# One of eight first-round passes computes its softmax on transposed scores

## The chip, the cores and the metric

The kernel runs on one core of one Trainium2 chip. The metric is the device time of one execution in microseconds; three runs of the kernel before gave 825.45, 827.18 and 828.26 us, so the median is 827.18 us. The engines are named as in the profile: PE (TensorE; PEld are its weight loads), DVE (VectorE), ACT (ScalarE), POOL (GpSimd), SP (SyncE, which issues the DMAs).

## The reference, cut to what matters

```python
# q, k, v: (4, 8, 1152, 64) float32; factor 2, scale 1/8
q_pool = q.reshape(B, H, 576, 2, 64).mean(axis=3)
scores = scale * np.matmul(q_pool, k.transpose(0, 1, 3, 2))      # 576 x 1152 for each head
scores = scores - np.max(scores, axis=-1, keepdims=True)
attn = np.exp(scores)
attn = attn / (np.sum(attn, axis=-1, keepdims=True) + 1e-09)
x = np.matmul(attn, v)                                           # heads side by side: (2304, 512)
out = ((x @ w_a) * (x @ w_b)) @ w_out                            # w_a, w_b: 512 x 1536; w_out: 1536 x 512
```

## The kernel before, in words

Attention is done in passes. A pass is one pair of heads of one batch, and the two heads lie in the two halves of the 128 partitions (64 dimensions each). Batch 0 is done in two rounds: four passes over the 256 "even" queries of each pair, then four over the other 320; the later batches take each pair in one pass. A block is 128 queries of one head: its scores are a row of 1152 numbers on each of 128 partitions, in the accumulator `sps`, which has room for the two heads' blocks and no more.

For a block, DVE scales the scores, takes the row maximum and copies them to a buffer `s` in one instruction (`sm_max`, L734); ACT writes exp(s - max) and the row sum (`sm_exp`, L741); DVE forms the reciprocal of the sum (L745, L751). What follows depends on the pass. In the first four passes (`N_PE = 4`, the first round of batch 0) the exponentials stay in float32: PE transposes them in 36 blocks of 128 x 128 a pass into the two accumulators `ab` (`tr_pe`, L776), ACT and DVE copy them out (`tr_out`, L787 and L789), PE multiplies them with v (`pv_f`, L820), and ACT and DVE divide by the sums with the help of a small diagonal matrix (`r_diag` L792, `r_wide` L796, `x_copy` L870, `r_mul` L800). In all later passes the probabilities are split into two float16 parts (L754, L758) and transposed by DMA.

Beside the first eight passes, all the weights are prepared. There are 36 tiles of 512 KB; each is loaded, two ACT instructions (`w_tail` L592, `w_abs` L573) and one on POOL (`w_sign` L596) take its bits apart, DVE joins them (`w_join` L603), its largest magnitude is found (`w_mag`, on ACT L582 or on DVE L585), PE adds the magnitudes over partitions into `xps` (`w_sum` L615), and ACT and DVE write a high and a low part (`w_hi` L639, `w_lo` L643 to L652). After the even round of batch 0 its 256 tokens go through the two expert products (`moe_mm` L944), which a last `w_sum` precedes on PE, and from then on attention of later batches alternates on PE with the expert tiles.

The order is not left to a scheduler: five lists of task numbers (`ORDERS`), one for each engine, give the sequence in which each engine executes its tasks, and each engine executes its queue strictly in order. `add` records what each task reads and writes, and a task waits until those before it on the same names are done.

Of the kernel before, what the change touches and what calls it, by code (L numbers as in the profile page):

```python
# [18 lines left out]
NP = H // 2  # L19
# [12 lines left out]
K_PART = 640  # L32
N_PE, EVICT = 4, "ADADA"
# [276 lines left out]
def kernel(  # L310
# [41 lines left out]
    osb = [T(f"o{u}", [128, DM]) for u in range(2)]  # L352
    z_t = osb + [T("z2", [128, 512])]
    one = T("one", [128, 1])
    vmx = T("vmx", [128, NPAIR])

    vsc = T("vsc", [128, NPAIR, 4])
    vb = T("vb", [128, B, 2])
# [847 lines left out]
```

## Time and profile before

| what | value |
|---|---|
| median of three runs | 827.18 us (825.45 to 828.26) |
| the profiled execution, whole | 824.38 us |
| its span, first to last instruction | 822.6 us |
| PE busy, mean granted clock | 782.5 us (95%), 0.979 |
| DVE busy | 615.3 us (75%) |
| ACT busy | 581.9 us (71%) |
| POOL busy | 246.6 us (30%) |

The shares are means over two very different stretches. The chain that ended last runs through PE for 74% of the span, but of the 40 slices of the profile (20.6 us each) PE is below 90% in the first six, and ACT and DVE are near full there. A granted clock of 1.00 is 2.4 GHz on TensorE and 0.50 is 1.2 GHz, so 0.75 over a stretch means half of it at the lower level.

### The profile page before, as it was taken

The numbers are of one execution on the slowest core, as the hardware profiler recorded it, in microseconds if no ns is written. First come the engines' busy times: TensorE is split into PE (matmuls) and PEld (weight loads), VectorE is DVE, ScalarE is ACT, GpSimd is POOL, SyncE is SP. The second block draws the span as 40 slices with busy tenths as digits, with TensorE's granted clock in tenths as the row PEclk, the third lists the DMA queues.
The fourth block names the chain that finished last, engine by engine and source line by source line (L and its number), as shares of the span: only waits on it lengthen the run. The fifth ranks groups of instructions, "written<-read, shape, count | busy, mean of one in ns | idle before, by whom it ended". The sixth has DMA issues, their size and how long they took to land.

```text
span 822.6 us, 21334 instructions
## 1 busy us (share of the span) xinstructions
PE 782.5 (95%) x8880; PEld 605.2 (74%) x8880; DVE 615.3 (75%) x1180; ACT 581.9 (71%) x986; POOL 246.6 (30%) x226
## 2 busy tenths in 40 slices
PE   8888569999999999999999999999999999999997
PEld 5665347776777767777777777887788888887886
DVE  5988999897799899999999999989977423022110
ACT  6999999887877788788887878778857452233212
POOL 5667876234201143111322023102300220402203
PEclk9988689999999999999999999999999999999999
DMA  8555688999999999999999999999958314000100
GB/s 306 205 199 182 194 212 254 185 209 222 202 200 221 214 201 190 199 201 217 202 209 195 174 159 190 193 186 186 182 103 141 76 43 100 2 27 1 27 2 26
DMA packets 316433, 132.32 MB, mean 161 GB/s; under 512 B 300848, under 2 KB 302896, under 8 KB 316336
## 3 DMA queue, kind: packets, MB, share of 16 engines
q1 hardware_dynamic: 316336, 130.96, 76.0%
q8 instruction: 69, 1.13, 0.6%
q14 instruction: 28, 0.23, 0.1%
HBM read 50.72 MB, written 4.72 MB: 67 GB/s over the span
## 4 chain that ended last, share of the span: by engine, by line
PE 74%; DVE 11%; ACT 8%; DMA 4%; issue 2%; SPq 1%; DVEq 0%; POOL 0%; ACTq 0%; POOLq 0%
PE ab L944 30%; PE ab L970 16%; PE xps L857 10%; PE sps L699 8%; PE sps L702 7%; DVE s L734 3%; DMA pt<-p 3%; DVE p L758 2%; ACT s L741 2%; PE xps L820 1%; ACT p L754 1%; DMA vraw<-in_v_dram 1%; DMA xt<-in_w_ab_dram 1%; ACT xt L592 1%; ACT pt L787 1%
## 5 line engine op out<-in xcount | busy, mean ns | idle before, releaser
L944 PEld LDWEIGHTS <-wab 128*128 128x128 f16 x2592 | 251.5, 98 | 32.7 <-issue 2.1
L944 PE MATMUL ab<-xt,wab 128*128 128x256 f16 x2304 | 260.7, 273 | 1.3 <-DVE o L976 0.8
L741 ACT ACTIVATE s<-s,st 128x1152 f32<-128x1152 f32 x144 | 180.0, 1250 | 28.9 <-DVE s L734 28.1
L758 DVE SCALAR_TENSOR_TENSOR p<-s,st,p 128x1152 f16<-128x1152 f32 x128 | 183.5, 1438 | 11.9 <-ACT p L754 11.5
L964 POOL TENSOR_TENSOR gl<-g,gh 128x256 fp32r<-128x256 f32 x108 | 90.1, 839 | 321.6 <-ACT gh L961 293.3
L754 ACT ACTIVATE p<-s,st 128x1152 f16<-128x1152 f32 x128 | 159.3, 1249 | 36.8 <-DMA pt<-p 11.4
L970 PE MATMUL ab<-wo,gh 128*128 128x512 f32 x432 | 139.5, 404 | 2.0 <-DVE g L956 1.7
L951 ACT ACTIVATE g<-ab,cc 128x256 f32<-128x256 f32 (+1 forms) x144 | 55.1, 415 | 83.7 <-PE ab L944 83.1
L734 DVE TENSOR_SCALAR_CACHE_REDUCE s<-sps,ksc 128x1152 f32<-128x1152 f32 x72 | 101.0, 1409 | 13.5 <-PE sps L702 13.1
L699 PE MATMUL sps<-k,q 64*128 64x512 f32 (+3 forms) x448 | 101.4, 546 | 9.6 <-DVE s L734 4.8
L956 DVE SCALAR_TENSOR_TENSOR g<-ab,cc,g 128x256 f32<-128x256 f32 (+1 forms) x144 | 55.2, 410 | 74.0 <-ACT g L951 73.8
L857 PEld LDWEIGHTS <-vs 128*64 128x64 f16 x3888 | 100.4, 110 | 13.0 <-issue 11.0
L857 PE MATMUL xps<-pt,vs 128*64 128x128 f16 (+1 forms) x3888 | 109.0, 215 | 0.7 <-DMA pt<-p 0.5
L734 DVE TENSOR_SCALAR_CACHE_REDUCE s<-sps 128x1152 f32<-128x1152 f32 x72 | 96.7, 1349 | 15.4 <-PE sps L699 14.5
L699 PEld LDWEIGHTS sps<-k,q 64*128 64x128 f32 (+1 forms) x448 | 47.6, 183 | 63.3 <-issue 53.2
L970 PEld LDWEIGHTS ab<-wo,gh 128*128 128x128 f32 x432 | 78.1, 188 | 20.5 <-issue 1.8
L970 PE MATMUL ab<-wo,gl 128*128 128x512 f32 x216 | 85.5, 396 | 1.0 <-POOL gl L964 1.0
L961 ACT ACTIVATE gh<-g 128x256 fp32r<-128x256 f32 x108 | 43.9, 411 | 55.3 <-PE ab L970 50.6
L702 PE MATMUL sps<-k,q 64*128 64x512 f16 (+3 forms) x624 | 65.5, 341 | 1.7 <-DVE s L734 1.6
L702 PEld LDWEIGHTS <-q 64*128 64x128 f16 (+1 forms) x720 | 36.7, 97 | 40.9 <-issue 8.3
L596 POOL TENSOR_SCALAR xt<-xt 128x512 f16<-128x512 f32 x22 | 51.9, 2360 | 27.1 <-ACT xt L592 20.8
L976 DVE COPY o<-ab 128x512 f32<-128x512 f32 x9 | 6.2, 687 | 64.0 <-PE ab L970 64.0
(124 smaller groups left out, 763.9 us busy)
## 6 DMA issues: line engine op xcount, KB each, us to landing
k<-in_k_dram SPq DMA_DIRECT2D x18, 576.0 KB, 4.6
vraw<-in_v_dram SPq DMA_DIRECT2D x17, 576.0 KB, 4.6
xt<-in_w_ab_dram SPq DMA_DIRECT2D x15, 512.0 KB, 3.8
qraw<-in_q_dram SPq DMA_DIRECT2D x12, 576.0 KB, 4.9
out_dram<-o SPq DMA_DIRECT2D x16, 256.0 KB, 2.9
xt<-in_w_out_dram SPq DMA_DIRECT2D x7, 512.0 KB, 3.7
g<-in_w_ab_dram SPq DMA_DIRECT2D x5, 512.0 KB, 3.3
wab<-in_w_ab_dram SPq DMA_DIRECT2D x4, 512.0 KB, 3.9
```

Of the source, the lines that this page charges most:

```text
L699: nc.tensor.matmul(out, q, k, start=True, stop=True)
L702: nc.tensor.matmul(out, q[:, hq], k[:, hk], start=(hq, hk) == (0, 0), stop=(hq, hk) == (1, 0))
L734: nc.vector.tensor_scalar(out=s_t[sbuf(i)], in0=sps[:, at:at + S], scalar1=-1.0 / 16.0 if u is None else ksc[:, u, 4:5], scalar2=None, op0 ...
L741: nc.scalar.activation(out=s, in_=s, func=AF.Exp, scale=-1.0, bias=t[:, 0:1], accum_out=t[:, 1:2])
L754: nc.scalar.activation(out=p_t[pbuf(i)][:, 0], in_=s_t[sbuf(i)], func=AF.Copy, scale=st_t[i % NST][:, 3:4])
L758: nc.vector.scalar_tensor_tensor(out=p[:, 1], in0=s, scalar=st_t[i % NST][:, 3:4], in1=p[:, 0], op0=ALU.mult, op1=ALU.subtract)
L857: nc.tensor.matmul(xps[half(e), at:at + w], vs[:, c, e, hv], pt[t][:, hp, c, c0:c0 + w], start=(c == 0 and n == 0), stop=(c == NCH - 1 and ...
L944: nc.tensor.matmul(dst if t < 8 else dst.rearrange("p (b n) -> p b n", b=B), wab[:, f, 1 - m, a, c], moe_x(t, b, c), start=(n == 0), stop= ...
L951: nc.scalar.activation(out=g_t[:, f, c], in_=ab[j][:, 1, c], func=AF.Copy, scale=cc[:, b, f, 0:1])
L956: nc.vector.scalar_tensor_tensor(out=g, in0=ab[j][:, 0, c], scalar=cc[:, b, f, 1:2], in1=g, op0=ALU.mult, op1=ALU.mult)
L964: nc.gpsimd.tensor_tensor(out=gl_t[j], in0=g_t[:, f], in1=gh_t[j].bitcast(F32), op=ALU.subtract)
L970: nc.tensor.matmul(acc[u], g[:, us], wo[:, f, a], start=(first and n == 0), stop=(last and n == 2))
```

## The change

The second pass of the first round (`T_PASSES = (1,)`, heads 2 and 3 of batch 0, even queries) gets a routine of its own, `t_pass`, in place of the four blocks. It still forms the four blocks of scores as before, but DVE only takes their maxima (`t_max`). Four small products with the identity lay the 4 x 128 maxima along the free dimension (`t_row`), and ACT keeps them in a row (`t_keep`). Then the scores are formed a second time, transposed, with keys on the partitions, in five groups (chunks of 128 keys: 2, 2, 2, 2, 1): for each chunk and head one product of k and q and one of a selecting matrix `sel` with the maxima, which subtracts the maximum in the accumulator (`t_s`). ACT writes the exponentials of a group out of both accumulators (`t_exp`), and these are the operands of p times v without any transpose; a product with ones forms the row sums in the other half of `xps` (`t_pv`, which begins with a product of zeros over all of `xps`). At the end ACT copies the sums, DVE takes reciprocals and multiplies (`t_sum`, `t_rec`, `t_out`). For this pass the 36 transposes and their copies, the exponentials by rows, the diagonals and `r_wide` are gone. The exponentials lie in the buffers `p` and in two of the six `pt` slots. POOL fills `sel` at the very start. All five order lists are new.

```diff
+T_PASSES, T_SLOTS = (1,), (4, 5)
...
+    def t_max(i):
+        at = S_AT[blocks[i].head]
+        nc.vector.tensor_reduce(out=st_t[i % NST][:, 0:1], in_=sps[:, at:at + S], axis=AX.X, op=ALU.max)
+
+    def t_row(i0):
+        for r in range(2):
+            for e in range(2):
+                m = st_t[(i0 + 2 * r + e) % NST][:, 0:1]
+                nc.tensor.matmul(
+                    xps[half(e), 128 * r:128 * r + 128], m.broadcast_to([128, 64]), ident, start=True, stop=True
+                )
+
+    def t_s(ps_, j, g):
+        for n, c in enumerate(GROUPS[g]):
+            for e in range(2):
+                nc.tensor.matmul(
+                    acc[e][:, TOK * n:TOK * n + TOK], kn[ps_.jk][half(e), 128 * c:128 * c + 128],
+                    qs[ps_.jq][half(e), 0:TOK], start=True, stop=False,
+                )
+            for e in range(2):
+                nc.tensor.matmul(acc[e][:, TOK * n:TOK * n + TOK], sel[half(e)], mrow[half(e)], start=False, stop=True)
+
+    def t_exp(j, g, e):
+        n = len(GROUPS[g])
+        nc.scalar.activation(
+            out=room(j, g, e)[0], in_=acc[e][:, 0:TOK * n], func=AF.Exp, scale=1.0 / 16.0
+        )
+
+    def t_pv(p, j, g):
...
+            for e in range(2):
+                nc.tensor.matmul(xps[half(e), 0:TOK], vf[p % 2][:, c, 64 * e:64 * e + 64], at[e][:, TOK * n:TOK * n + TOK], start=False, stop=False)
+            for e in range(2):
+                nc.tensor.matmul(xps[half(e), TOK:2 * TOK], one.broadcast_to([128, 64]), at[e][:, TOK * n:TOK * n + TOK], start=False, stop=stop)
...
+        add("PE", 0.5, i - 10, t_row, (ps_.base,), r=[f"st{k % NST}m" for k in range(ps_.base, i)] + ["g0"], w=["xps"], mode=2)
+        add("ACT", 0.27, i - 4, t_keep, (j,), r=["xps"], w=["g4"])
+        for g, of in enumerate(GROUPS):
...
+            add("PE", 0.04 + 0.88 * w, i - 7 + g / 5, t_s, (ps_, j, g), r=kq_names(ps_) + ["g3", "g4"], w=["acc0", "acc1"], mode=1)
...
+        if m in T_PASSES:
+            t_pass(ps_, m)
```

ACT's queue at the second pass, before. L787 are copies of transposes, L741 exponentials, L792 diagonals, L870 the copy of p times v, and the lines on `wab`, `z`, `g` and `xt_64` are weights:

```order
L787 ACTIVATE pt_71<-ab_105 128x512
L792 ACTIVATE g<-g,st 128x128
L741 ACTIVATE s_82,st<-s_82,st 128x1152
L592 ACTIVATE wab<-wab 128x512
L573 ACTIVATE z_96<-g 128x512
L592 ACTIVATE g<-g 128x512
L582 ACTIVATE wab,wmx<-wab 128x512
L787 ACTIVATE pt_72<-ab_105 128x512
L592 ACTIVATE xt_64<-xt_64 128x512
L741 ACTIVATE s_80,st<-s_80,st 128x1152
```

The same queue now, up to the first exponentials of the transposed pass (L855 is `t_keep`, L869 `t_exp`, L753 an exponential of the third pass, L651 `w_hi`, L603 `w_tail`, L988 the split of the first pass's result):

```order
L651 ACTIVATE wab<-o_95,wsc 128x512
L593 ACTIVATE wab,wmx<-wab 128x512
L651 ACTIVATE wab<-o_94,wsc 128x512
L584 ACTIVATE o_95<-wab 128x512
L651 ACTIVATE wab<-wab,wsc 128x512
L855 ACTIVATE g<-xps 128x256
L603 ACTIVATE xt_64<-xt_64 128x512
L988 ACTIVATE xt_63<-x_66 128x256
L753 ACTIVATE s_82,st<-s_82,st 128x1152
L869 ACTIVATE p_86<-ab_106 128x512
L869 ACTIVATE p_86<-ab_107 128x512
```

Weight conversions now stand where the second pass had its exponentials and copies, and `t_keep` follows them.

PE's queue at the second pass, before: the pass's last scores (`k_73,q_79`), transposes into `ab`, two `w_sum` (L615), and the third pass's scores (`k_74,q_78`) between them:

```order
L699 MATMUL sps<-k_73,q_79 128x128
L776 MATMUL ab_106<-g,s_80 128x128 x4
L615 MATMUL xps<-wmx,one 128x2
L776 MATMUL ab_105<-g,s_80 128x128 x4
L615 MATMUL xps<-wmx,one 128x2
L699 MATMUL sps<-k_74,q_78 128x512 x4
L699 MATMUL sps<-k_74,q_78 128x128
```

PE's queue now, from the same last scores to the first of the transposed ones (L627 is `w_sum`, L850 `t_row`, L860 and L865 `t_s`):

```order
L711 MATMUL sps<-k_73,q_79 128x128
L627 MATMUL xps<-wmx,one 128x2 x2
L711 MATMUL sps<-k_74,q_78 128x512 x4
L711 MATMUL sps<-k_74,q_78 128x128
L627 MATMUL xps<-wmx,one 128x2
L850 MATMUL xps<-g,st 64x128 x4
L860 MATMUL ab_106<-q_79,k_73 128x256
L860 MATMUL ab_107<-q_79,k_73 128x256
L865 MATMUL ab_106<-g 128x256
```

The small products with the maxima stand behind the third pass's first scores and behind a third `w_sum`.

## Rows read from the trace of the kernel before

**Rows 1.** Busy time by stretch: range, length, PE, PEld, DVE, ACT, POOL, clock, DMA.

```profile
8.27:38.00 29.73, 26.06 (x208) 18.42 (x207) 26.89 (x62) 29.41 (x62) 21.62 (x11) 1.00 0.77 283
38.00:61.70 23.70, 19.36 (x147) 14.52 (x146) 20.49 (x47) 21.75 (x46) 16.41 (x10) 0.86 0.53 184
61.70:95.00 33.30, 26.76 (x177) 16.32 (x176) 30.02 (x68) 32.32 (x64) 27.80 (x16) 0.81 0.57 195
95.00:121.40 26.40, 13.52 (x116) 8.75 (x114) 25.82 (x47) 24.60 (x46) 19.90 (x10) 0.72 0.82 204
121.40:200.00 78.60, 76.72 (x976) 57.75 (x974) 67.85 (x120) 67.51 (x108) 32.61 (x25) 1.00 1.03 215
200.00:700.00 500.00, 497.24 (x6404) 386.91 (x6405) 424.78 (x777) 371.60 (x563) 101.13 (x115) 1.00 0.93 175
```

**Rows 2.** Chain that ended last, before the expert products: start, us, engine, tile, line.

```profile
119.75 1.23 ACT wab L582 x4
121.03 0.38 PE xps L615 x2
```

**Rows 3.** Timeline of ACT: start, length, engine, line, operation, shapes.

```profile
30.94 1.25 ACT L741 ACTIVATE s<-s,st 128x1152 f32<-128x1152 f32 x1
...
32.18 0.36 ACT L870 ACTIVATE x<-xps,vsc 128x128 f32<-128x128 f32 x1
32.43 0.69 ACT L792 ACTIVATE g<-g,st 128x128 f32<-128x128 f32 x2
33.02 0.43 ACT L787 ACTIVATE pt<-ab 128x128 f32<-128x128 f32 x2
33.33 0.68 ACT L592 ACTIVATE xt<-xt 128x512 int32<-128x512 uint32 x1
33.90 0.42 ACT L894 ACTIVATE xt<-x 128x256 f16<-128x256 f32 x1
34.20 0.59 ACT L787 ACTIVATE pt<-ab 128x512 f32<-128x512 f32 x1
34.68 1.34 ACT L639 ACTIVATE wab<-o,wsc 128x512 f16<-128x512 f32 x2
```

**Rows 4.** Timeline of ACT, an exponential's high part and its successor.

```profile
98.55 1.29 ACT L754 ACTIVATE p<-s,st 128x1152 f16<-128x1152 f32 x1
99.69 0.69 ACT L573 ACTIVATE o<-xt 128x512 f32<-128x512 f32 x1
```

**Rows 5.** Timeline of DVE, end of the second pass's maxima.

```profile
28.59 1.36 DVE L734 TENSOR_SCALAR_CACHE_REDUCE s<-sps 128x1152 f32<-128x1152 f32 x1
...
30.60 0.68 DVE L789 COPY pt<-ab 128x512 f32<-128x512 f32 x1
31.19 0.67 DVE L585 TENSOR_REDUCE wmx<-o 128x1 f32<-128x512 f32 x1
...
31.86 0.69 DVE L603 SCALAR_TENSOR_TENSOR z<-z,g 128x512 int32<-128x512 int32 x1
32.57 0.29 DVE L800 SCALAR_TENSOR_TENSOR x<-x,xps 128x128 f32<-128x128 f32 x1
32.78 1.35 DVE L734 TENSOR_SCALAR_CACHE_REDUCE s<-sps 128x1152 f32<-128x1152 f32 x1
```

**Rows 6.** Timeline of PE at the full clock, second pass.

```profile
26.36 2.20 PE L699 MATMUL sps<-k,q 64*128 64x512 f32 x10 [0.40 <-DVE s L734]
...
28.49 1.09 PE L776 MATMUL ab<-g,s 128*128 128x128 f32 x8
...
29.51 2.19 PE L820 MATMUL xps<-pt,vs 128*64 128x128 f32 x36
...
31.52 0.39 PE L796 MATMUL xps<-g,one 128*64 128x128 f32 x4
```

**Rows 7.** Timeline of PE, the same two products later.

```profile
52.28 3.66 PE L820 MATMUL xps<-pt,vraw 128*64 128x128 f32 x36
...
65.03 4.15 PE L699 MATMUL sps<-k,q 64*128 64x512 f32 x10 [0.15 <-DVE s L734]
```

More of the change, by code (lines that the diff above doesn't have):

```diff
@@ L396, with room @@
     ptf = [x.rearrange("p a c n -> p (a c n)").bitcast(F32).rearrange("p (c n) -> p c n", c=NCH) for x in pt]
+    sel, mrow, rsum = g_t[:, 3, 0:128], g_t[:, 4], g_t[:, 5]
+    GROUPS = [range(c, min(c + 2, NCH)) for c in range(0, NCH, 2)]
+    spare = [(x.rearrange("p a n -> p (a n)").bitcast(F32), [f"p{j}h", f"p{j}l"]) for j, x in enumerate(p_t)]
+    spare += [(pt[j].rearrange("p a c n -> p (a c n)").bitcast(F32), [f"pt{j}"]) for j in T_SLOTS]
+    spare = [(x[:, 512 * n:512 * n + 512], names) for x, names in spare for n in range(2)]
+    def room(j, g, e):
+        x, names = spare[2 * g + e if g < 4 else 8]
+        return x[:, 256 * e:256 * e + 256] if g == 4 else x, names
     vf = [vs.rearrange("p c e h d -> p (c e h d)").bitcast(F32).rearrange("p (c n) -> p c n", c=NCH), vraw]
@@ new lines, in t_keep @@
+    def t_keep(j):
+        nc.scalar.activation(out=mrow, in_=xps[:, 0:TOK], func=AF.Copy)
+    def t_s(ps_, j, g):
[7 more added lines that the diff above has]
+                nc.tensor.matmul(acc[e][:, TOK * n:TOK * n + TOK], sel[half(e)], mrow[half(e)], start=False, stop=True)
@@ new lines, in t_exp @@
+    def t_exp(j, g, e):
[4 more added lines that the diff above has]
+    def t_pv(p, j, g):
+        at = [room(j, g, e)[0] for e in range(2)]
+        if g == 0:
+            for e in range(2):
+                nc.tensor.matmul(
+                    xps[half(e)], zero.broadcast_to([128, 64]), zero.broadcast_to([128, 2 * TOK]), start=True, stop=False
+                )
+        for n, c in enumerate(GROUPS[g]):
+            stop = c == NCH - 1
+            for e in range(2):
+                nc.tensor.matmul(xps[half(e), 0:TOK], vf[p % 2][:, c, 64 * e:64 * e + 64], at[e][:, TOK * n:TOK * n + TOK], start=False, stop=False)
+            for e in range(2):
+                nc.tensor.matmul(xps[half(e), TOK:2 * TOK], one.broadcast_to([128, 64]), at[e][:, TOK * n:TOK * n + TOK], start=False, stop=stop)
@@ new lines, in t_sum, with t_rec, t_out, t_pass @@
+    def t_sum():
+        nc.scalar.activation(out=rsum, in_=xps[:, TOK:2 * TOK], func=AF.Copy, bias=1e-9)
+    def t_rec():
+        nc.vector.reciprocal(out=rsum, in_=rsum)
+    def t_out(p, j, x0):
+        nc.vector.scalar_tensor_tensor(
+            out=x32[j][:, x0:x0 + TOK], in0=xps[:, 0:TOK], scalar=vb[:, p // NP, 1:2] if p % NP == NP - 1 else vsc[:, p, 0:1], in1=rsum, op0=ALU.mult, op1=ALU.mult
+        )
+    def t_pass(ps_, n):
+        j, i, p = 0, ps_.base, ps_.p
+        for rows, *_ in ps_.todo:
+            for e in range(2):
+                scores(ps_, i, rows, e)
+                ps_.last_max = add("DVE", 1.27, i - 4, t_max, (i,), r=[f"sps{e}"], w=[f"st{i % NST}m"])
+                i += 1
+        add("PE", 0.5, i - 10, t_row, (ps_.base,), r=[f"st{k % NST}m" for k in range(ps_.base, i)] + ["g0"], w=["xps"], mode=2)
+        add("ACT", 0.27, i - 4, t_keep, (j,), r=["xps"], w=["g4"])
+        for g, of in enumerate(GROUPS):
+            w = len(of)
+            add("PE", 0.04 + 0.88 * w, i - 7 + g / 5, t_s, (ps_, j, g), r=kq_names(ps_) + ["g3", "g4"], w=["acc0", "acc1"], mode=1)
+            for e in range(2):
+                add("ACT", 0.06 + 0.21 * w, i - 4 + g / 5, t_exp, (j, g, e), r=[f"acc{e}"], w=[f"room{j}{g}{e}"])
+            add("PE", 0.04 + 0.88 * w + 0.25 * (g == 0), i - 9 + g / 5, t_pv, (p, j, g), r=[f"room{j}{g}{e}" for e in range(2)] + [x for e in range(2) for x in room(j, g, e)[1]] + vbuf(p) + ["ones"],
+                w=["xps"], mode=2)
+        add("ACT", 0.27, i - 5, t_sum, (), r=["xps"], w=["g5"])
+        add("DVE", 0.33, i - 5, t_rec, (), w=["g5"])
+        add("DVE", 0.4, i - 5, t_out, (p, ps_.jx, XE), r=["xps", "g5", f"vb{p // NP}" if p % NP == NP - 1 else f"vsc{p}"], w=[f"x32{ps_.jx}{c}" for c in range(XE // 64, (XE + TOK) // 64)])
+        x_split(ps_, ("even",), i - 4)
@@ L1095 @@
     add("POOL", 0.8, -30, unity, (), w=["g0"], port=False)
+    add("POOL", 0.6, -25, select, (), w=["g3"], port=False)
     for n in range(IDLE):
@@ L1111, in attend @@
             prep_qk(nxt, nxt.base - 6)
+        if m in T_PASSES:
+            t_pass(ps_, m)
+            if nxt and not nxt.again:
+                prep_vmax(nxt.p, nxt.parts[0] == "even", ps_.end - 4)
         i = ps_.base
-        for r, (rows, (at, w), leaving, splits) in enumerate(ps_.todo):
+        for r, (rows, (at, w), leaving, splits) in enumerate(ps_.todo if m not in T_PASSES else ()):
             slots = []
```

5 lines of the change are left out of this document (added), and 287 rows, old and new, of the table ORDERS.

## The prediction, made before the changed kernel ran

> **What bounds the kernel now.** I read the busy times by stretch first. From 121.4 to 700 us PE is busy 574.0 of 578.6 us at a clock of 1.00, so whatever starts the expert products earlier or later moves the end by as much. Before 121.4 us PE is busy in parts only and the clock falls to 0.72. ACT is the fullest engine there: 29.41 of 29.73 us, then 21.75 of 23.70, 32.32 of 33.30 and 24.60 of 26.40; it waits 5.05 us of 113.1 from its first instruction at 8.27 us. DVE is near full too but waits 9.9 us in the same four rows [rows 1]. The chain of waits names the hand-over: ACT takes two weight magnitudes until 120.98, PE adds them up and starts the expert products at 121.4 [rows 2]. So the question is when ACT has worked off its queue up to that last magnitude. ACT executes in order; a wait early in the queue is not made good by work that stands behind it.
>
> **The change part by part.** I take the cost on ACT as the distance from one start to the next, since its instructions overlap at the ends: an exponential of 1152 is 1.24 us, a copy of p times v 0.25, a diagonal 0.295, a pair of small copies 0.31, a weight conversion 0.57, a 512-wide copy out of an accumulator 0.48, a high weight part 0.61 [rows 3], a high part of 1152 is 1.14 [rows 4].
>
> ACT loses 4 exponentials (4.96), 4 wide copies (1.92), 2 pairs of small ones (0.62), 4 diagonals (1.18) and 2 copies of p times v (0.50): 9.2 us. It gains 8 exponentials 512 wide, 2 of 256 and two copies of 256. No row shows an exponential out of an accumulator: the wide copy (0.48) bounds it from below, 512/1152 of 1.24 from above (0.55). I take 0.50, nearer to the copy, 0.30 for 256: 5.2 us, 5.0 to 5.6. Net **-4.0 us of ACT work** ahead of the expert products.
>
> DVE's four maxima stay at one pass over 1152 each (1.29 from 28.59 to the next) [rows 5]; what goes is 4 wide copies of 0.60, small sums and products, about 3.5, and a reciprocal and a product of 256 come in. No row shows a wide reciprocal. At DVE's rate of 1152 in 1.29 us the two take about 0.65; if a reciprocal is several times slower per element, 2.5. I take 0.7, since nothing but the pass's own result waits for it. Net -2.8.
>
> PE loses 36 transposes (0.13 each, from 28.49 to 29.51 for 8), two p times v (2.01) and two `r_wide` (0.3): 9.3 us [rows 6]. Five score products of 2176 columns in all take 2.13 us, 0.98 ns a column. The pass adds 36 products of 256 columns in `t_s` and as many in `t_pv`: 9.0 us each at that rate, 8.0 at that of p times v (18 x 128 columns in 2.01). With `t_row` and the zeros it is 17.5 to 18.7; if the two heads' products did not overlap in the new shapes it would be twice that. I take 18. Net **+8.7 us of PE**, in a stretch where PE is busy 45.4 of 53.4 us up to 61.7 [rows 1]. It costs nothing by itself: ACT is the limit and PE has room; the cover goes where ACT waits for a group. The POOL fills lie ahead of the first q sum, in the wait for its load; SP issues the same loads in a new order.
>
> If ACT waited as long as now, its 4.0 us less would be the gain. But the new routine adds a wait in front of everything it does: **no exponential can be formed before all four maxima are taken**, where the old pass started each block's exponential after its own maximum. I walk through the queues with the durations above.
>
> *First wait.* The scores of a pass come block after block, because `sps` holds two, and between the maxima DVE still has the first pass's copies and the joins. The third and fourth maximum start at 28.6 and 32.8 now [rows 5]. With the new order I get 29.5 and 32.8, so the fourth again ends at 34.1. DVE's 22.0 us of work up to there would allow 29, but PE and DVE wait for each other over `sps`. Behind the last maximum PE's queue has, ahead of `t_row`, the third pass's scores (2.1) and a `w_sum` that waits for two magnitudes on DVE (about 37.5, behind a join that needs ACT). So `t_row` ends at 38.4 and `t_keep` starts at 38.65. ACT's queue up to it holds 14 weight conversions, 4 exponentials, 6 magnitudes and high parts, 8 copies of transposes, 4 diagonals and 2 of p times v: 20.85 us. From 8.27 it could be through at 29.1. **It waits 9.5 us where it now waits 0.3** in that stretch [rows 1].
>
> *Second wait.* From `t_keep` to `t_sum` ACT has 19.8 us to do (11 conversions, 7 weight parts, 3 exponentials of the third pass, the 10 of this one, 2 copies, a split). Each group of `t_s` (1.8 us) writes both accumulators, so it waits for both exponentials of the group before, and these stand between weight work in ACT's queue. PE in the same time has 18 us of this pass, the third pass's scores (2.6) and transposes (1.8). Walking both queues I find 2.6 us in which ACT waits for a group. `t_sum` ends at 61.75.
>
> *What is left.* From there to the last magnitude before the expert products ACT's queue holds 33 conversions, 11 exponentials of 1152, 6 other passes over 1152, 23 weight parts and magnitudes, 8 diagonals, 4 copies of p times v, 3 splits and 14 copies of transposes: 61.6 us. Now ACT does 56.9 us from 61.7 to 121.4 and waits 2.8 [rows 1]. So it is **4.7 us behind**. I give back 1.8 of the 2.8 us of waits, since an engine that is behind finds what it needs ready more often, and DVE has some 3 us less to do; 1.0 stays. The last magnitude then ends at 124.4 against 120.9, and the expert products start 3.5 us later.
>
> From there both orders hold the same work on PE, which is full [rows 1], so the 3.5 us reach the end. The profiled execution took 824.38 us (span 822.6); it would be 827.9. It lies 2.8 us under the median of the three runs, and I carry that over: **830.7 us**. The waits give the forecast's own range: with none in the transposed stage the shift is 0.9, with all of 2.8 kept it is 5.3, and an error of 1.5 us in the walk comes on top, so 828.5 to 834.
>
> **The rivals.** *The gain is kept.* The order lists put the stage where ACT has other work at hand, ACT waits 5 us in all as now, and the 4.0 us come through: 823.2. For it: ACT was full and is the engine relieved. Against it: the order puts 20.85 us of ACT work in front of `t_keep`, and the fourth maximum cannot come much before 34.
>
> *A wash.* The first wait is as I say or a few us shorter, the stage runs without waits, and ACT later never waits: work left at the sums 2 us smaller than I count, shift about 0: 827. For it: the four rows sum to only 5.05 us of ACT waits now, so a well-packed queue is possible. Against it: DVE is at 95% or more over 95 to 121 and would have to be ahead.
>
> *The clock falls in the transposed stage* and the change costs much more. Now, whenever PE works in pieces with waits between, the same products take 3.66 us instead of 2.19 and 4.15 instead of 2.20 [rows 6, 7], and the clock of that stretch is 0.86. The new stage is such work: five groups of 1.8 us, each waiting for two exponentials. If half of its 18 us ran at 1.2 GHz, the groups on ACT's path would grow by about 4.5 us in all: 835. Against it: PE has more to do there than now, and where it is full the clock is 1.00. The Trainium skill, TensorE: Matmul & The Clock Gate, section "A second HAM failure mode: psum-queue depth-cycling", says that a PE that cycles through PSUM banks and idles shortly between groups oscillates between its two clocks; by that rule this rival would be the likely one, and the trace agrees so far as its pieces of work between 52 and 69 us ran at the low level.
>
> **How the numbers follow.** A measurement of this kernel tells a change of about 0.3% (2.5 us) from none. Forecast: 0.52, seven eighths of it over 829.7. Gain kept: 0.17. Wash: 0.25, all of it within 0.3%. Fallen clock: 0.06. So faster is 0.17, same 0.25 and an eighth of 0.52, 0.32, and slower the rest of 0.52 and 0.06, 0.51. The range runs from 824 to 834.5: it leaves out most of the gain and the upper half of the fallen clock, under 2 in 10.
>
> **What would show it.** In the changed kernel's profile: `t_keep` near 38.6 us with ACT idle 8 to 10 us before it, released by PE's products with the maxima; the sums' copy near 62; two waits or more of ACT for PE inside the stage; the expert products from 124 to 126; PE full and at 1.00 from there. I am wrong if ACT's idle time up to the start of the expert products stays under 8 us, or if that start comes at 121.4 or earlier. If the start is as I say and the end isn't, then PE was not what bound the rest.

## The result: 11.3 us slower, and the profile after

The changed kernel took 837.93 us in the median (837.01 to 840.40, four executions) against 826.62 us for the kernel before on the same chip (825.45 to 828.26, four). The recorded ratio is 1.0142, with a 95% interval of 1.0117 to 1.0167 (it is not the ratio of the two medians, which is 1.0137). I had forecast 3.5 us slower and a range that ended at 834.5. The direction was right; the size was not, and the time lies outside the range. The rivals that kept the gain or made it a wash are out. The profiled execution took 837.39 us, its span is 835.6 us (before 822.6): 13.0 us more.

Busy time by stretch of the changed kernel, columns as in [rows 1]; the last row is the stretch from the sums of the new pass to the first expert product.

```profile
8.27:38.00 29.73, 24.40 (x179) 16.32 (x178) 26.30 (x51) 21.25 (x43) 17.31 (x9) 0.94 0.59 217
38.00:61.70 23.70, 22.58 (x182) 15.20 (x181) 15.27 (x24) 20.13 (x40) 16.41 (x9) 1.00 0.54 187
61.70:95.00 33.30, 25.11 (x190) 16.83 (x188) 30.88 (x73) 30.66 (x64) 23.13 (x14) 0.95 0.48 168
95.00:121.40 26.40, 13.65 (x84) 9.29 (x80) 26.01 (x49) 25.39 (x46) 19.04 (x10) 0.61 0.84 244
...
200.00:700.00 500.00, 493.70 (x6324) 381.28 (x6323) 425.76 (x778) 373.63 (x567) 104.87 (x118) 1.00 0.93 176
61.70:128.60 66.90, 44.46 (x327) 29.88 (x324) 64.09 (x129) 63.00 (x123) 48.30 (x26) 0.82 0.68 203
```

Read against [rows 1]: ACT is idle for 8.5 us of the first row (before 0.3), as forecast; up to the keep it is 10.0. In the second row PE is at the full clock (before 0.86), and DVE has fallen from 20.49 to 15.27 us, which I had not forecast. From there to the expert products DVE is busy 64.09 of 66.90 us, more than ACT. And between 200 and 700 us PE now waits 6.3 us where it waited 2.8.

Timeline of ACT: the last conversion ahead of the keep, `w_hi`, the keep (L855), the copy of the sums (L888). In brackets stands the idle time before, and what ended it.

```profile
34.59 0.68 ACT L584 ACTIVATE o<-wab 128x512 f32<-128x512 f32 x1
37.34 0.72 ACT L651 ACTIVATE wab<-wab,wsc 128x512 f16<-128x512 f32 x1 [2.08 <-DVE wsc L635]
39.54 0.38 ACT L855 ACTIVATE g<-xps 128x256 f32<-128x256 f32 x1 [1.48 <-PE xps L850]
...
62.13 0.38 ACT L888 ACTIVATE g<-xps 128x256 f32<-128x256 f32 x1
```

Timeline of PE: the third pass's scores at the low clock (they answer to [rows 7]), the weight sum, the row of maxima, and the hand-over to the expert products (L1038), which answers to [rows 2].

```profile
34.38 3.90 PE L711 MATMUL sps<-k,q 64*128 64x512 f32 x10
38.20 0.38 PE L627 MATMUL xps<-wmx,one 128*128 128x2 f32 x2
38.84 0.66 PE L850 MATMUL xps<-g,st 128*64 128x128 f32 x8 [0.25 <-DVE wsc L630]
...
128.35 0.38 PE L627 MATMUL xps<-wmx,one 128*128 128x2 f32 x2 [1.09 <-ACT wab L593]
128.60 2.78 PE L1038 MATMUL ab<-xt,wab 128*128 128x256 f16 x24
```

Timeline of DVE: the first maximum of all, the two long waits of the transposed stage, and the reciprocal of the sums.

```profile
8.02 1.36 DVE L746 TENSOR_SCALAR_CACHE_REDUCE s<-sps 128x1152 f32<-128x1152 f32 x1 [7.13 <-PE sps L711]
...
44.26 0.69 DVE L614 SCALAR_TENSOR_TENSOR o<-o,xt 128x512 int32<-128x512 int32 x1 [3.55 <-issue]
...
50.88 1.20 DVE L655 SCALAR_TENSOR_TENSOR wab<-o,wsc,wab 128x512 f16<-128x512 f32 x1 [3.57 <-ACT wab L651]
...
62.55 1.75 DVE L891 RECIPROCAL g<-g 128x256 f32<-128x256 f32 x1 [0.52 <-ACT g L888]
```

The same first maximum before, on DVE:

```profile
7.05 1.36 DVE L734 TENSOR_SCALAR_CACHE_REDUCE s<-sps 128x1152 f32<-128x1152 f32 x1 [6.19 <-PE sps L699]
```

It starts 1.0 us later in the profile after, before any work of the new pass. The fills on POOL are not the reason (they end 2.7 us ahead of the first q sum); what is late is the first scores, which wait for loads, and SP's list is new as well: a third weight load now stands ahead of the load of v. Over the seven kernels of the table below that have the changed kernel's list of loads up to there, itself among them (1, 3, 4, 6, 7 and 8), this maximum lies at 8.02 to 10.63 us (mean 9.56), over the four with the list of before, itself among them (2, 5 and 9), at 7.05 to 8.68 (mean 7.94). The two ranges overlap. So the new order of the loads probably costs a part of it; it was not tried apart. The other two parts of the 13.0 us: from the first maximum to the first expert product 6.3 us more (120.6 against 114.3), and from there to the end 5.7 us more (707.0 against 701.3), where I had forecast none.

Right behind the pass the next ten score products ran at the low clock, and DVE's next maximum waited for them:

```profile
65.62 3.70 PE L711 MATMUL sps<-k,q 64*128 64x512 f32 x10 [1.52 <-POOL q L435]
69.36 1.36 DVE L746 TENSOR_SCALAR_CACHE_REDUCE s<-sps 128x1152 f32<-128x1152 f32 x1 [1.59 <-PE sps L711]
```

### The profile page after: what moved, and what is told of

Read it like the earlier page. It is cut to its first block, busy times and chain, and to the rows that moved or that the text cites. A ratio compares the mean times of both kernels' runs of the same rounds, so it can differ in the third digit from the quotient of the medians.

```text
span 835.6 us, 21396 instructions
## 1 busy us (share of the span) xinstructions
PE 789.9 (95%) x8918; PEld 608.6 (73%) x8918; DVE 618.3 (74%) x1165; ACT 578.3 (69%) x976; POOL 240.6 (29%) x229
## 4 chain that ended last, share of the span: by engine, by line
PE 52%; DVE 5%; DMA 4%; issue 2%; ACT 1%; SPq 1%; DVEq 0%; ACTq 0%
PE ab L1038 23%; PE ab L1064 14%; PE sps L714 7%; PE xps L951 6%; DMA pt<-p 3%; DVE s L746 2%; PE sps L711 2%; DVE p L770 1%; DMA vraw<-in_v_dram 1%; DMA k<-in_k_dram 1%; ACT p L766 1%; SPq L775 1%; DVE vmx L511 0%; DVE g L1050 0%; ACT s L753 0%
## 5 line engine op out<-in xcount | busy, mean ns | idle before, releaser
L1038 PEld LDWEIGHTS <-wab 128*128 128x128 f16 x2592 | 251.2, 98 | 32.2 <-issue 1.7
L1038 PE MATMUL ab<-xt,wab 128*128 128x256 f16 x2304 | 261.0, 273 | 1.1 <-DVE o L1070 0.8
L1058 POOL TENSOR_TENSOR gl<-g,gh 128x256 fp32r<-128x256 f32 x108 | 95.5, 889 | 344.4 <-ACT gh L1055 314.0
L753 ACT ACTIVATE s<-s,st 128x1152 f32<-128x1152 f32 x140 | 174.7, 1248 | 27.4 <-DVE s L746 27.0
L951 PE MATMUL xps<-pt,vs 128*64 128x128 f16 (+1 forms) x3888 | 110.7, 215 | 5.1 <-DMA pt<-p 4.4
L746 DVE TENSOR_SCALAR_CACHE_REDUCE s<-sps 128x1152 f32<-128x1152 f32 x68 | 91.3, 1349 | 16.7 <-PE sps L711 15.9
L435 POOL TENSOR_TENSOR q<-qraw 128x576 f32<-128x576 f32 (+2 forms) x20 | 26.1, 1304 | 81.8 <-PE sps L711 38.8
```

The lines of the kernel that those rows point to most:

```text
L746: nc.vector.tensor_scalar(out=s_t[sbuf(i)], in0=sps[:, at:at + S], scalar1=-1.0 / 16.0 if u is None else ksc[:, u, 4:5], scalar2=None, op0 ...
L753: nc.scalar.activation(out=s, in_=s, func=AF.Exp, scale=-1.0, bias=t[:, 0:1], accum_out=t[:, 1:2])
L951: nc.tensor.matmul(xps[half(e), at:at + w], vs[:, c, e, hv], pt[t][:, hp, c, c0:c0 + w], start=(c == 0 and n == 0), stop=(c == NCH - 1 and ...
L1038: nc.tensor.matmul(dst if t < 8 else dst.rearrange("p (b n) -> p b n", b=B), wab[:, f, 1 - m, a, c], moe_x(t, b, c), start=(n == 0), stop= ...
L1058: nc.gpsimd.tensor_tensor(out=gl_t[j], in0=g_t[:, f], in1=gh_t[j].bitcast(F32), op=ALU.subtract)
```

## Experiments

The table holds what was read from each profiled execution (first maximum on DVE, first expert product on PE, time from there to the end of the span), and the median with its recorded ratio to the kernel before on the same chip. Medians of different rows can be from different chips; the kernel before took 825.53 to 826.86 us on them. Where a kernel leaves out or adds instructions, its paragraph says which; the others differ in order alone, or in where the row of maxima stands. Behind the first expert product 1, 8, 13, 14, 16 and 17 have the lists of before, as 5, 9, 11 and 15 have; the changed kernel, 2, 3, 4, 6, 7, 10 and 12 have the new ones.

| kernel | first maximum | first expert product | from there | span | median | ratio (95%) |
|---|---|---|---|---|---|---|
| before | 7.05 | 121.3 | 701.3 | 822.6 | 826.62 | |
| changed | 8.02 | 128.6 | 707.0 | 835.6 | 837.93 | 1.0142 (1.0117 to 1.0167) |
| 1 changed, old lists behind | 9.52 | 128.7 | 702.0 | 830.7 | 833.70 | 1.0097 (1.0060 to 1.0134) |
| 2 before, new lists behind | 8.46 | 121.9 | 705.1 | 827.0 | 829.27 | 1.0045 (1.0024 to 1.0066) |
| 3 no division | 8.16 | 127.4 | 706.1 | 833.5 | 837.91 | 1.0145 (1.0103 to 1.0186) |
| 4 row early | 9.81 | 129.1 | 705.2 | 834.3 | 839.47 | 1.0176 (1.0129 to 1.0222) |
| 5 pv three times | 8.68 | 131.0 | 701.6 | 832.6 | 832.85 | 1.0082 (1.0059 to 1.0105) |
| 6 t_pv twice | 10.19 | 140.3 | 707.8 | 848.1 | 846.02 | 1.0262 (1.0242 to 1.0282) |
| 7 no select | 10.60 | 129.2 | 704.5 | 833.7 | 838.04 | 1.0151 (1.0125 to 1.0177) |
| 8 no select, old lists behind | 10.63 | 130.7 | 702.0 | 832.7 | 835.70 | 1.0116 (1.0094 to 1.0138) |
| 9 pv of one chunk | 7.57 | 121.7 | 704.3 | 826.0 | 827.63 | 1.0033 (1.0014 to 1.0052) |
| 10 changed, re-sorted | 8.12 | 114.6 | 715.5 | 830.1 | 833.84 | 1.0076 (1.0050 to 1.0102) |
| 11 before, re-sorted | 8.31 | 120.4 | 710.9 | 831.3 | 829.47 | 1.0034 (1.0009 to 1.0059) |
| 12 row, re-sorted | 7.70 | 116.6 | 710.2 | 826.8 | 830.64 | 1.0057 (1.0037 to 1.0077) |
| 13 as 10, old lists behind | 8.39 | 115.0 | 712.9 | 827.9 | 831.68 | 1.0063 (1.0041 to 1.0084) |
| 14 changed, sorted for delays | 8.79 | 120.8 | 708.4 | 829.2 | 829.33 | 1.0032 (1.0013 to 1.0051) |
| 15 before, sorted for delays | 8.50 | 119.1 | 712.3 | 831.4 | 832.04 | 1.0071 (1.0048 to 1.0094) |
| 16 row, sorted for delays | 8.02 | 123.1 | 707.4 | 830.5 | 832.46 | 1.0076 (1.0060 to 1.0093) |
| 17 as 12, old lists behind | 8.49 | 119.9 | 712.3 | 832.2 | 828.92 | 1.0032 (1.0012 to 1.0053) |

The times inside a row are of one execution, which can lie some us from the median (834.03 us in 17, whose median is 828.92). How well they repeat can be read from kernels with the same lists. From the first maximum to the first expert product the changed kernel needs 120.6 us and 1, with the same head, 119.1; the kernel before needs 114.3 and 2 113.4. Behind it the kernel before, 1, 5, 8 and 9 need 701.3 to 704.3 us (mean 702.2), and the changed kernel, 2, 3, 4, 6 and 7 need 704.5 to 707.8 (mean 706.0). So a difference of some 1.5 us up to the start, or of some 3 us behind it, is not told by a single pair.

**1 and 2: the lists behind the first expert product.** Both kernels have the same tasks there; only their order differs. The two hybrids exchange it. The first differing line of PE's list, in 1:

```diff
-        469, 470, 714, 490, 561, 557, 722, 562, 558, 732, 565, 566, 569, 740, 516, 570, 574, 575, 578, 579, 582, 757,
+        469, 470, 714, 490, 561, 557, 722, 562, 558, 732, 565, 566, 569, 516, 570, 740, 574, 575, 578, 579, 582, 757,
```

and in 2:

```diff
-        461, 462, 487, 488, 732, 508, 579, 575, 740, 580, 576, 750, 583, 584, 587, 534, 588, 758, 592, 593, 596, 597,
+        461, 462, 487, 488, 732, 508, 579, 575, 740, 580, 576, 750, 583, 584, 587, 758, 534, 588, 592, 593, 596, 597,
```

Expected of 1: 

> The changed kernel with its own order up to the first expert product; from there each engine follows the lists of the kernel before. The changed kernel loses 5.8 us behind that point (707.0 us from the first expert product to the end of the span, 701.2 before). If the new order of the rest costs them: first expert product near 128.6 as in the changed kernel, 701 us from there, so 829.8 of span and about 832 in all. If they come from what the transposed pass leaves behind (work of DVE and ACT that is late at that point): 707 us from there, 837 to 838.

Expected of 2: 

> The kernel before with its old pass and its own order up to the first expert product; from there each engine follows the lists of the changed kernel. If the new order of the rest costs 5.8 us: first expert product at 121.4, 707 us from there, 832 in all. If it is the transposed pass that leaves work behind: 701 us from there, 826.6.

Measured: the changed kernel gets back 5.0 of its 5.7 us, the kernel before loses 3.8. The new lists cost this, not what the pass leaves behind, since 2 has no new pass. PE's waits behind the first expert product (what waited, for whom: us, times, longest) show where. The changed kernel:

```profile
PE xps L951 <- DMA pt<-p: 4.4, 6, 1.4
```

The changed kernel with the old lists behind (1):

```profile
PE xps L951 <- DMA pt<-p: 0.9, 2, 0.7
```

The kernel before, and the kernel before with the new lists behind (2), where the line is L857:

```profile
PE xps L857 <- DMA pt<-p: 0.5, 1, 0.5
```

```profile
PE xps L857 <- DMA pt<-p: 3.4, 4, 1.5
```

p times v of the later passes waits for probabilities that are transposed by DMA; in the new order these come too late, 3.5 us in all in one pair and 2.9 in the other. Medians agree less sharply (4.2 us gained, 2.7 lost), but with both signs, and the two means above lie 3.7 us apart; 5.7 and 5.0 are the upper end.

**3: the wide reciprocal.**

```diff
-        nc.vector.reciprocal(out=rsum, in_=rsum)
+        nc.vector.tensor_scalar(out=rsum, in0=rsum, scalar1=2.0 ** -20, scalar2=None, op0=ALU.mult)
```

> The changed kernel with the reciprocal of 256 sums replaced by a product with a constant of the same shape, so that pass's result isn't divided. The reciprocal took 1.75 us on DVE, such a pass about 0.35. If DVE is what limits the stretch from 61.7 us to the expert products (it is busy 30.9 of 33.3 and 26.0 of 26.4 us there), they start 1.4 us earlier, at 127.2. If ACT limits it, as the prediction took it, the start stays at 128.6 within 0.3. The time alone cannot tell 1.4 us; the start is read from the profile.

On DVE the product of the same shape took

```profile
62.93 0.57 DVE L891 TENSOR_SCALAR g<-g 128x256 f32<-128x256 f32 x1 [0.52 <-ACT g L888]
```

which is 1.18 us less than the reciprocal (I had put it at 0.35 us, not 0.57), and the first expert product came 1.2 us earlier. But that is not shown to be the reciprocal's doing. From the start of this instruction to the first expert product 3 needs 64.5 us; 1, 4 and 6, which keep the reciprocal, need 64.7, 64.5 and 64.5. Only the changed kernel (66.1) and 7 and 8 (66.1 and 65.7) need more, and in these three the ten scores right behind the pass ran at the low clock and DVE waited 1.6 to 1.7 us for them. In 1 they ran at the full clock and DVE did not wait:

```profile
67.04 2.17 PE L711 MATMUL sps<-k,q 64*128 64x512 f32 x10 [1.53 <-issue]
69.46 1.35 DVE L746 TENSOR_SCALAR_CACHE_REDUCE s<-sps 128x1152 f32<-128x1152 f32 x1
```

3 itself has a wait of 0.5 us for later scores at the low clock, which can hide that much. So what a shorter reciprocal is worth stays open; the time shows nothing either, as it cannot at this size. The run does not show that DVE alone bounds the stretch. In 1, DVE is idle for 0.7 of these 64.7 us and ACT for 2.3, and the chain that ended last runs over ACT from 70.9 to 110.8 us and over DVE from there to 128.4: both are full, and they hand over to each other.

**4: the maxima sooner.**

```diff
-                    xps[half(e), 128 * r:128 * r + 128], m.broadcast_to([128, 64]), ident, start=True, stop=True
+                    sps[half(e), S + 128 * r:S + 128 * r + 128], m.broadcast_to([128, 64]), ident, start=True, stop=True
...
-        nc.scalar.activation(out=mrow, in_=xps[:, 0:TOK], func=AF.Copy)
+        nc.scalar.activation(out=mrow, in_=sps[:, S:S + TOK], func=AF.Copy)
```

with `t_row` and the first `t_s` moved ahead on PE, the keep and the first exponentials on ACT. 

> The changed kernel with the row of maxima formed in 256 free columns of the scores' accumulator, so that it need not wait for the weight sums: its products stand right behind the last maximum on PE, the keep and the first two groups' work stand ahead of the weight's high part on ACT. The keep then comes at about 34.8 instead of 39.5 us. If the wait for the four maxima sets the loss, as the prediction took it, the expert products come 3 to 4 us earlier, near 125, and the time is about 834. If DVE's queue behind it sets the start, it moves by less than 1 us and the time stays at 837 to 838.

The keep came early and the time did not fall. ACT's timeline shows why:

```profile
35.85 0.38 ACT L855 ACTIVATE g<-sps 128x256 f32<-128x256 f32 x1
...
39.76 1.09 ACT L869 ACTIVATE p<-ab 128x512 f32<-128x512 f32 x2 [0.18 <-PE ab L865]
44.14 1.26 ACT L753 ACTIVATE s<-s,st 128x1152 f32<-128x1152 f32 x1 [3.29 <-DVE s L746]
```

The third pass's scores now stood behind the transposed ones, so the exponential of the third pass waited instead. The sums came at 64.2 us, no earlier than in the changed kernel once the later first maximum is taken off (54.4 us behind it, against 54.1). The run shows that the wait moved, not what it would be worth to remove it.

**5 and 6: PE work added in the stage.** In 5, the kernel before forms p times v of the second pass three times over:

```diff
-        for c in range(NCH):
+        for _ in range(3 if p == 1 else 1):
+            for c in range(NCH):
```

> The kernel before, every list as it was; its second pass forms each of its two products of probabilities and v three times over (the same result), which adds 4 times 2.0 us of PE work at the full clock to the stretch where the changed kernel adds 8.7, and no work to any other engine. If PE has room there, as the prediction took it, 826 to 828 and the expert products at 121.4 to 122.5. If extra PE work in that stretch goes through to the end, 832 to 835.

In 6, the changed kernel forms each product of exponentials with v and with ones twice:

```diff
-        for n, c in enumerate(GROUPS[g]):
-            stop = c == NCH - 1
+        for n, c, again in [(n, c, x) for n, c in enumerate(GROUPS[g]) for x in range(2)]:
+            stop = c == NCH - 1 and again == 1
```

> The changed kernel, every list as it is; each product of exponentials with v and with ones is formed twice, so numerator and denominator double and the quotient is the same. That adds 9 times 0.87 = 7.8 us of PE work to the transposed stage. If PE's work in that stage goes through to the end: 844 to 847. If the new lists leave PE room there (taking 3.9 us away gave nothing): 838 to 841.

Counted from the first maximum, the start moved by 8.1 us in 5 (122.3 against 114.3) and by 9.5 in 6 (130.1 against 120.6); the times rose by 7.3 us against the kernel before on the same chip (825.59) and by 8.1 against the changed kernel. In 6 the stretch from the keep to the copy of the sums, which is 22.6 us in the changed kernel, in 1 and in 3 alike, took 31.5. All of the added PE work went through. Busy time of 38 to 61.7 us, in 5:

```profile
38.00:61.70 23.70, 20.69 (x198) 17.86 (x200) 17.35 (x38) 17.02 (x35) 13.84 (x9) 0.78 0.42 147
```

and in 6:

```profile
38.00:61.70 23.70, 22.99 (x146) 15.24 (x148) 11.10 (x22) 15.39 (x28) 12.68 (x6) 0.81 0.41 141
```

ACT falls from 21.75 to 17.02 and from 20.13 to 15.39, DVE from 20.49 to 17.35 and from 15.27 to 11.10: what PE does longer there, both do later (the window stands still, so a part of each fall is the first maximum, 1.6 and 2.2 us later in these two). From the first expert product on, 5 needs 701.6 us and 6 needs 707.8, each within what its own lists need without the added work.

**7, 8 and 9: PE work taken out.** 7 and 8 leave out the products that subtract the maxima in the accumulator:

```diff
-            for e in range(2):
-                nc.tensor.matmul(acc[e][:, TOK * n:TOK * n + TOK], sel[half(e)], mrow[half(e)], start=False, stop=True)
```

> The changed kernel, every list as it is, without the products of the selecting matrix and the row of maxima, so the maxima aren't subtracted before the exponentials (the row and the wait for it stay). That takes 9 times 0.43 us of PE work out of the transposed stage. If the PE work goes through to the end, 837.9 falls to about 834; if it is hidden, 837 to 838.5 and the expert products at 128.6 within 0.5.

> The same omission in the changed kernel that follows the lists of before from the first expert product on (833.7 us). If the PE work goes through to the end, about 830; if it is hidden, 833 to 834.5.

9 is the kernel before with one key chunk in place of nine in the second pass's p times v:

```diff
-        for c in range(NCH):
+        last = 1 if p == 1 else NCH
+        for c in range(last):
```

> The kernel before, every list as it was, but its second pass multiplies only the first of nine key chunks with v, so that pass's result is a partial sum. That takes 2 times 1.8 us of PE work at the full clock out of the stretch where the changed kernel adds 8.7, and leaves ACT and DVE as they were. If PE is on the path there (as the run with the products three times over says), the expert products start 3 to 4 us earlier and the time is 822 to 823.5. If PE has room there and the tripled products cost only because they went past it, 825 to 827.

None of the three is faster than the kernel it was made from: 7 is level with the changed kernel, 8 is 2.0 us above 1, with intervals that overlap, and 9 is 2.1 above the kernel before on its chip (825.53). In 7, counted from the first maximum, the start came 2.0 us earlier (118.6), but only 0.5 earlier than in 1 (119.1), which has the same head and keeps the products. The stage itself is the sharper measure: from the keep to the copy of the sums 7 and 8 need 21.5 us instead of 22.6, so 1.1 of the 3.9 us taken out came through. The timeline of PE in 7 has a reason why a part of the rest is given back: PE had waited 1.38 us for ACT, the granted clock from 38 to 61.7 us is 0.93 where it was 1.00, and groups of four products that took 0.60 us take 1.07 in places. In 7:

```profile
44.27 1.81 PE L860 MATMUL ab<-q,k 64*128 64x256 f32 x8 [1.38 <-ACT p L867]
46.01 0.64 PE L875 MATMUL xps<-zero 128*64 128x512 f16 x2
46.44 1.07 PE L881 MATMUL xps<-p,vraw 128*64 128x256 f32 x4
47.29 1.07 PE L883 MATMUL xps<-p,one 128*64 128x256 f32 x4
```

In the changed kernel the same products with v and with ones:

```profile
45.28 0.60 PE L883 MATMUL xps<-p,vraw 128*64 128x256 f32 x4
45.72 0.60 PE L885 MATMUL xps<-p,one 128*64 128x256 f32 x4
```

So in this stage more PE work costs its full price in either order, and less gains little (1.1 of 3.9 us in the new order, nothing to be seen in the old one): PE is at the edge, with no room left, and below the edge something else is as late.

**10 to 12: other lists for all of it.** Is the loss in the pass or in its lists? A local search moved tasks a few places in their queues, as long as a replay of the queues ended earlier; tasks and dependences stayed. First differing line of PE's list in 10:

```diff
-        3, 4, 5, 22, 6, 23, 7, 8, 29, 37, 49, 35, 41, 39, 55, 43, 9, 10, 17, 65, 67, 162, 45, 164, 71, 69, 46, 166,
+        3, 4, 5, 6, 7, 8, 22, 23, 9, 29, 10, 35, 37, 49, 39, 41, 17, 55, 43, 65, 67, 162, 45, 46, 164, 69, 63, 71, 73,
```

> The changed program, every task, buffer and dependence as it is, with the five order lists re-sorted: tasks were moved a few places in their queue as long as a replay of the queues ended earlier. The wait for all four maxima, the wide reciprocal and the transposed groups stay. If the lists cost most of the 11.3 us: the expert products start at 118 to 122 us where they started at 128.6, 701 to 704 us follow, 821 to 828 in all. If the pass itself costs them (its waits for maxima and for groups, its work on DVE), the start stays at 126 or later and the time at 833 or above.

> The control: the kernel before, with its old pass, re-sorted by the same search with the same effort. If its lists were already as good as this search gets, 825 to 827 as before. If the search improves any list, the expert products start 2 to 5 us earlier than 121.4 and the time is 821 to 824; then the pass is worth the difference between this run and the re-sorted changed kernel.

> The changed program with the row of maxima in free columns of the scores' accumulator, so that it does not wait for weight sums, re-sorted in the same way. If the place of the row in the accumulator of the weight sums costs anything that a better order can't hide, the expert products start 1 to 3 us before those of the re-sorted changed kernel; if not, both start within 1 us of each other.

10 starts its expert products at 114.6 us, 14.0 us earlier than the changed kernel with the same tasks, waits and reciprocal. So the pass does not force the late start. But its time falls by only 4.1 us: 715.5 us follow instead of 707.0. Busy time of 10 in the stage, and after the start:

```profile
38.00:61.70 23.70, 22.94 (x180) 15.72 (x179) 19.00 (x32) 23.27 (x47) 17.86 (x10) 1.00 0.52 182
128.60:200.00 71.40, 65.31 (x877) 47.92 (x876) 62.88 (x113) 60.81 (x93) 23.61 (x20) 1.00 1.06 202
```

DVE is no longer starved in the stage (19.00 against 15.27). But a good half of the 14.0 us is work put off: up to the first expert product DVE has been busy for 98.06 us instead of 106.00, and ACT for 99.17 instead of 106.33. PE then waits 6.1 us between 128.6 and 200 (2.1 in the changed kernel), 3.8 of them for DVE and 2.2 for a transpose by DMA. The control, 11, is 3.2 us above the kernel before: the search improves its own replay, not the chip's time.

**13 to 17: with the old lists behind, and sorted for delays.** 13 and 17 take the re-sorted heads of 10 and 12 with the old lists behind; 14 to 16 were searched again with instructions randomly prolonged in the replay, 14 from the lists of 13, so that it and 16 have the old lists behind as well. The first differing line in 13:

```diff
-        469, 470, 714, 561, 557, 562, 558, 565, 566, 722, 569, 490, 570, 732, 516, 574, 578, 579, 575, 740, 757, 582,
+        469, 470, 714, 561, 557, 562, 558, 565, 566, 722, 569, 490, 732, 516, 570, 740, 574, 575, 578, 579, 582, 757,
```

> The re-sorted changed kernel up to some 10 us behind the first expert product, then the lists of the kernel before. The re-sorted kernel started its expert products at 114.6 us and needed 715.5 us from there; the lists of before need 701 to 702. If the start moves the end one to one, as the prediction took it, 114.6 and 702 make 816.6 of span and 818 to 820 in all. If the early start only came by putting off weight work that the expert products then wait for, the rest stays above 708 us and the time at 825 or more.

> The changed program again, every task and dependence as it is, its head re-sorted from the lists of the run before this one in the list, with the replay of the queues repeated under disturbed durations (DVE, ACT and POOL instructions longer by random amounts), so that an order counts only if it stands delays. If the pass is worth nothing by itself and the lists made the loss: 825 to 828, as before. If the pass itself costs (maxima, reciprocal, PE's 9 us more): 831 or more.

> The control: the kernel before, re-sorted with the same disturbed replay, starting from its own lists. Expected within 2.5 us of 826; the difference of the changed program to this run is what the pass is worth at equal care for the order.

> The changed program with the row of maxima in free columns of the scores' accumulator (no wait for weight sums), re-sorted with the same disturbed replay. If the row's place in the accumulator of the weight sums is worth something, 1 to 3 us below the changed program re-sorted the same way, 823 to 826, the lowest of all; if not, within 1.5 us of it.

> The re-sorted changed kernel with the row of maxima in the scores' accumulator (830.6 us, the least idle time of PE of all runs, 34.9 us), which from some 25 us behind the first expert product on follows the lists of the kernel before. If the lists of before are worth 3 to 5 us there, as they were with the changed kernel's own head, 826 to 828, level with the kernel before. If they fit only what they were made with, 830 to 832.

13 refutes the rule that the start sets the end: it starts 6.3 us before the kernel before and ends 5.3 us behind it. PE's waits in 13 from 115 to 200 us:

```profile
PE sps L711 <- DVE s L746: 3.9, 2, 3.3
PE ab L1038 <- DVE g L1050: 3.2, 2, 3.0
```

14 brings the changed program from 837.93 to 829.33 us by order alone; some 4 us of that are the old lists behind, as 1 measures them. The old pass stands 2.7 us above it (15 against 14) or 4.4 below it (11 against 10), but neither pair is like for like: 14 was searched twice and 15 once, and 10 has the new lists behind where 11 has the old. With the old lists behind both, and one search each, the old pass is ahead by some 2.4 us (ratios 1.0034 in 11 and 1.0063 in 13, whose intervals overlap). What the pass is worth by itself stays open, its sign too. No version beat the kernel before: every interval lies above 1, and the nearest with the new pass are 14 and 17, at 1.0032. The row in the scores' accumulator gained 3.2 us once (12 against 10) and lost 3.1 the other time (16 against 14), so nothing follows for it.

## Why the prediction was wrong

**Right.** *First wait*: the keep came at 39.54 us (forecast 38.65), and ACT waited 10.0 us up to it (forecast 9.5). In part that is luck. The first maximum was 1.0 us late, and what held PE up ahead of the last weight sum was not the magnitudes on DVE, which ended at 37.24 (forecast 37.5), but the third pass's scores, which took 3.90 us at the low clock where I had 2.1. *Second wait*: ACT waited 2.1 us for groups (forecast 2.6). The copy of the sums ended at 62.51 (forecast 61.75), so up to here the walk holds. *The clock* of the stage is 1.00, so that rival is out as I put it. But the clock fell just ahead of the stage and just behind it, on the third pass's scores and on those of 65.62 us, and in 1, 4 and 6 the latter ran at the full clock. The Trainium skill's section "A second HAM failure mode: psum-queue depth-cycling" ("TensorE: Matmul & The Clock Gate") tells of a kernel that goes round PSUM banks with short idle times and swings between the two levels. The changed kernel's stage does not agree with that; with the selecting products left out (7) a part of it ran at the low level. I had also read [rows 7] too simply: between its two slow pieces the scores at 56.09 us took 2.20, at the full clock.

**Failed first: "What is left", in its waits.** ACT's work was near: from the end of the sums' copy to the last magnitude (62.51 to 128.35 us) it was busy for 62.1 us (forecast 61.6). But I had left it 1.0 us of waits, and it waited 3.75. What ACT waited for in that stretch (us in all, times, longest):

```profile
ACT pt L799 <- PE ab L788: 1.6, 1, 1.6
ACT wab L651 <- DVE st L757: 1.0, 1, 1.0
ACT s L753 <- DVE s L746: 0.9, 1, 0.9
```

The first stands behind the scores at the low clock, and 1 does not have it (2.3 us of waits in all). The others are waits for DVE, 2.1 us with a small third one. I had given back 1.8 us because "DVE has some 3 us less to do", and DVE had more. It was busy for 64.09 us in that stretch where it had been for 55.84 before [rows 1], 8.3 more, against 6.1 more on ACT. Of this, 5.8 us is work that it had not been able to do: it was busy 5.2 us less in the stage and 0.6 less ahead of it. In the stage it waited 3.55 us ahead of a join and 3.57 for a high part that stands behind new exponentials in ACT's queue. The rest is work that I had at -2.8 us up to the start and that came out at +2.4 (105.66 against 103.22); `t_rec` and `t_out` are 1.5 of that error, and some of the same instructions took longer (last section). So I walked one queue where two were full. The waits were 2.75 us more than forecast here and 1.3 more in 1, so the size differs between executions. That DVE's starvation in the stage is the lists' and not the pass's, 10 shows.

**Failed within it: the reciprocal.** I took 0.7 us for `t_rec` and `t_out` "since nothing but the pass's own result waits for it". They took 1.75 and 0.47. The argument was a poor one, since DVE works in order and was full, but no run shows that the 1.5 us reached the start (3).

**Failed as a statement, not in the sum: PE's 8.7 us "cost nothing by itself: ACT is the limit and PE has room".** PE's 8 us of idle time up to 61.7 us were not room. DVE and ACT get their next input from the same PE queue: 8 us added to either kernel there moved the start by 8.1 and 9.5 us (5, 6). The sum did not miss it, because the walk carried PE's work into ACT's waits and the sums came nearly when it said; and 3.6 us taken out of the kernel before brought the start no earlier (9).

**Failed: "From there both orders hold the same work on PE, which is full, so the 3.5 us reach the end."** Same work, but another order: 5.7 us more behind the start, 5.0 of which the old lists give back (1), most of it waits for transposes by DMA. Over the eleven profiles with either lists and no re-sorted head it is 3.7 us. I had read that all five lists were new and looked only at what they held before the expert products. Within one set of lists the rule did hold to within some 3 us: 701.6 us in 5 and 707.8 in 6, with the start 9.7 and 11.7 us later. Across lists it fails altogether (10, 13).

The sum, on the profiled executions: 1.0 us up to the first maximum (forecast 0: "SP issues the same loads in a new order"), 6.3 up to the first expert product (forecast 3.5), 5.7 behind it (forecast 0). Some 1.5 of the 6.3 are the wait behind the scores at the low clock, which the same lists do not always have.

## What to carry to other kernels

When an order is rewritten, check the whole of it: what stands behind the changed stage can cost as much as the stage, and exchanging the lists of two versions piece by piece on the chip finds it quickly. Walk every in-order queue that is near full, not only the fullest, and count as late whatever an engine could not do while it was starved. An early start of the long stretch is a milestone, not the end: it only counts if nothing that the stretch needs was put off for it. And before one microsecond in a profile is credited to an edit, look at a profile of a kernel with the same lists and without the edit.

## What the runs showed of the hardware

A reciprocal of 128x256 took 1.75 us on DVE, a product of that shape 0.57, and a reciprocal of 128x1 0.15 to 0.16. From these two sizes the reciprocal costs about 6 ns for each element of a partition (an estimate), and at one element that does not show.

The same join can take much longer on DVE beside POOL. By line and form up to the first expert product (count, busy us, mean ns), in the changed kernel:

```profile
L614 DVE SCALAR_TENSOR_TENSOR o<-o,wab 128x512 int32<-128x512 int32 x2 | 2.5, 1236 | 0.1
```

In the kernel before the mean is 676 ns. One of the two joins, and POOL at that time:

```profile
58.27 1.78 DVE L614 SCALAR_TENSOR_TENSOR o<-o,wab 128x512 int32<-128x512 int32 x1
```

```profile
57.88 1.61 POOL L664 TENSOR_TENSOR wo<-o,wo 128x512 fp32r<-128x512 f32 x1 [2.29 <-ACT wo L651]
59.45 1.20 POOL L435 TENSOR_TENSOR q<-qraw 128x256 f32<-128x256 f32 x1
```

The join ends 0.56 us after POOL's first product, and alone it takes 0.68. POOL's second product begins while the join still runs and takes 1.20 us; the same product at 4.17 us, with no join beside it, took 0.72. The Trainium skill, "SBUF — State Buffer", section "SBUF: two separate sides", says that DVE with two operands from SBUF and GpSimd take turns on a shared pair of ports; the trace agrees in this place. It was not tried apart.

Fewer products can be slower ones: without the selecting products, groups of PE in the stage took 1.07 us instead of 0.60 behind a wait of 1.38 us for ACT (7).
